# Results turned by VectorE in 32x32 blocks and stored in 128-byte runs; preparations split later

## The chip, the cores and the metric

One core of a Trainium2 chip. The metric is the device time of one execution in microseconds (us). The kernel before took 1075.37 us in the median of 3 runs (1073.84 to 1076.38). Engines: TensorE (PE in the profile, PEld for its weight loads), VectorE (DVE), ScalarE (ACT), GpSimd (POOL), SyncE (SP, which here only issues transfers).

## The reference, cut

```python
# q, k, v: (4, 8, 768, 64); gamma is one number for each head
for t in range(S):
    state = gamma * state + outer(k[t], v[t])
    y[t] = scale * q[t] @ state
x = y.transpose(0, 2, 1, 3).reshape(3072, 512)
h = x @ moe_w_in                                  # 512 -> 2048
x = maximum(0.01 * h, h) @ moe_w_out              # 2048 -> 512
h = x @ moe2_w_in
return (h * sigmoid(1.702 * h)) @ moe2_w_out      # (3072, 512) float32
```

A decayed linear attention, then two feed-forward layers, all in float32.

## The kernel before

The work runs in five stages, one after another on PE.

1. `retention()`: the attention, with the first block of the first input product between its steps (0 to 134 us of the trace).
2. The block loop: blocks 1 to 5 of the first input product. A block is 512 tokens, a tile `m` is 12 matmuls of 128x512 (`ffn_in`, L238) into one of six PSUM banks, and ACT empties the bank (L242). A call `later.tick()` ends a tile. Each float32 operand is kept as a rounded high part and a low part: ACT copies the high part, DVE subtracts (`split`, L154 and L151). `x_split(q, k)` does this for a quarter of the next block's input; it reads `x_raw`, and after the last quarter it issues the load of the block after (`x_load`, L205). In the same loop 36 weight preparations run (`Prep`), one started about every 1.78 tiles. A preparation loads its raw weights at tick 0, ACT and DVE turn them into float32 words and sums at tick 3 (`words`, `sums`: L172, L173, then L176 to L191 and L151). The first six (`keep`) and six later ones (`split`) also make the high and low parts at tick 4; stores go out at tick 6. The buffers for the sums, `rings[1]`, are three, so the words of the third preparation after one write where its sums stood.
3. `second1.run`: the first output product, 7 products in place of 8 for each 2x2 block (`Second`, L770).
4. `first2.run`: the second input product with the gate (`First`, L581).
5. `second2.run`: the second output product, three blocks of 56 items; an item is 6 matmuls of 128x512 (L770) with one `(blk, i, q)`. Operands are made four items ahead (`high` on ACT, L727; `low` on DVE, L151) in a ring of five tiles, so ACT may write the operand of an item once PE is done with the item five before. Raw rows are loaded 13 items ahead (`load`, L715, 256 KB each); sums of raw rows are made by DVE in the order of a table (`total`, L739).

A finished result of stage 5 is a tile `t` of 128 features by 2 x 512 tokens, so it is turned before it is stored. `evacuate` names four results for each block, S10, S11, S01 and S00 here, for (r, col) = (1,0), (1,1), (0,1), (0,0); they are turned at the ticks of items 43, 45 and 51 of their block and of item 1 of the next. Before the change `result2` has PE turn eight 128x128 pieces against `ident` into the PSUM banks of the result's tag (L994), ACT copies the banks to SBUF (L998), and one tick later SP issues one store of 512 KB with runs of 1 KB (L999). The last result of all goes through `last_result` (L1024 to L1036) and is not touched. Eleven results go through `result2`.

An SP instruction is issued in program order: a store that waits for its data holds the loads behind it. The tiles that hold results come from a ring of four (`second2.u`).

Of the kernel before, what the change touches and what calls it, by code (L numbers as in the profile page):

```python
# [21 lines left out]
P = 128  # L22
# [65 lines left out]
def retention_two_ffn(ctx: ExitStack, tc: tile.TileContext, qkv, consts, small, w1i, w1o, w2i, w2o, scratch, out):  # L88
    nc = tc.nc
    sbuf = ctx.enter_context(tc.tile_pool(name="sbuf", bufs=1, reuse_waits="tile"))  # L90
    banks = ctx.enter_context(tc.tile_pool(name="psum", bufs=1, space=PSUM)).tile([P, 8, TB], F32, name="psum")
# [24 lines left out]
    def run_of(area, n, step, at=0):  # L116
        return [(area, at + step * k) for k in range(n)]
# [11 lines left out]
    later = Later()  # L129
# [23 lines left out]
    def split(hi, lo, src, eng=nc.vector):  # L153
        nc.scalar.copy(out=hi, in_=src)  # L154
        subtract(lo, src, hi.bitcast(F32), eng)
# [48 lines left out]
    def x_load(q):  # L204
        nc.sync.dma_start(out=x_raw, in_=xd0[q])  # L205

    def x_split(q, k):
        split(xs[q % 2][k][:, 0], xs[q % 2][k][:, 1], x_raw[:, k])
        if k == NP - 1 and q + 1 < NB:
            x_load(q + 1)  # L210
# [20 lines left out]
    def ffn_in(blk, m, place=None):  # L231
        h = banks[:, h_banks[i_h[0] % len(h_banks)]]
        i_h[0] += 1
        w = wt[m].rearrange("p s (k f) -> p s k f", k=NP)
        i = 0
        for k in range(NP):
            for a, c in ((0, 1), (0, 0), (1, 0)):
                nc.tensor.matmul(out=h, lhsT=w[:, a, k], rhs=xs[blk % 2][k][:, c], start=(i == 0),  # L238
                                 stop=(i == 3 * NP - 1), skip_group_check=True)
                i += 1  # L240
        t = next(g_ring) if place is None else place
        nc.scalar.activation(out=t, in_=h, func=AF.Lrelu)  # L242
        if place is None:
            nc.scalar.dma_start(out=gd1[m][:, blk * TB : blk * TB + TB], in_=t)
# [159 lines left out]
    class Prep:  # L404
# [37 lines left out]
        def store(self):  # L442
            nc.sync.dma_start(out=wd[self.kind][:, self.q, self.hh], in_=self.t[:, 1:])
# [14 lines left out]
        def start(self, clock):  # L458
            self.load()
            split = self.kind == "2i" and self.q < N_SPLIT  # L460
            keep = self.kind == "1o" and self.q < 3
            clock.at(3, self.words)
            clock.at(3, self.sums)
            if split or keep:
                clock.at(4, self.split if split else self.keep)
            if not keep:
                clock.at(6, self.store_split if split else self.store)

        def steps(self):

# [14 lines left out]
    def w_load(kind, q, a, b):  # L485
        if kind == "2i" and q < N_SPLIT:
            nc.sync.dma_start(out=slot(q)[:, :, :, a:b], in_=wds[:, q, :, :, a:b])
        else:
            nc.sync.dma_start(out=slot(q)[:, :, 1, a:b], in_=wd[kind][:, q, :, a:b])
# [9 lines left out]
    def w_split(q, a, b):  # L499
        for hi, lo in w_parts(q, a, b):  # L500
            split(hi.bitcast(F32R), lo.bitcast(F32R), lo)
# [15 lines left out]
    class First:  # L517
# [46 lines left out]
        def run(self, done, step, behind):  # L564
# [9 lines left out]
            def product(t, n, i, start):  # L574
                blk, q = pairs[n]
                x = self.of[blk, i]
                w = slot(q).bitcast(F32R)[:, :, :, SLOTS["i"].index(i)]
                m = 0
                for k in range(2):
                    for a, b in ((0, 1), (0, 0), (1, 0)):  # L580
                        nc.tensor.matmul(out=t, lhsT=w[:, k, a], rhs=x[:, b, k], start=(start and m == 0),  # L581
                                         stop=(m == 5), skip_group_check=True)
                        m += 1
# [288 lines left out]
    for blk in range(1, NB):  # L872
        for m in range(KF):
            n = (blk - 1) * KF + m
            if given < min(N_IN1, (n + 1) * N_IN1 // 64):
                Prep(*names[given], prep_rings).start(later)
                given += 1
            if blk + 1 < NB:
                if m in (8, 9, 10, 11):
                    x_split(blk + 1, m - 8)  # L880
            elif m == 11:
                second1.begin(later, 2 * NQ, 2 * NQ, 3, 1)
            ffn_in(blk, m, second1.place(0, 1, *divmod(m, NQ)) if blk + 1 == NB else None)
            if blk + 1 == NB and m in freed:
                q = freed[m]
                for a, b in ((3, 7), (0, 3)) if m < 11 else ((6, 7), (3, 6), (0, 3)):
                    w_load("1o", q, a, b)
                if m < 11:
                    later.at(3, lambda q=q: w_split(q, 3, 7))
                    later.at(4, lambda q=q: w_split(q, 0, 3))  # L890
            later.tick()
# [14 lines left out]
    def done1(n, blk, i, q):  # L906
# [19 lines left out]
        if i == 2 and q < 3:  # L926
# [8 lines left out]
    second2 = Second({"x": run_of(x_a, 8, 2), "y": run_of(y_a, 8, 2), "z": run_of(z_a, 8, 2),  # L935
                      "ops": run_of(o_a[0], 4, 4) + run_of(o_a[1], 1, 4),
                      "u": run_of(u_a[0], 2, 4) + run_of(u_a[1], 2, 4)},
                     gd2, {"d": (4, 5), "e": (6, 7), "f": (0, 1), "h": (2, 3)})
# [42 lines left out]
    ident = Area("g").view(0, P)  # L981
# [4 lines left out]
    def result2(blk, r, col, t, tag, ticks=2):  # L986

        def turn():
            b0 = second2.p_banks[tag][0]
            y = banks[:, b0 : b0 + 2].rearrange("p j (b f) -> p (j b) f", f=2 * P).rearrange(  # L990
                "p b (j f) -> p b j f", j=2)
            for b in range(4):
                for j in range(2):
                    nc.tensor.matmul(out=y[:, b, j], lhsT=t[:, j, b * P : b * P + P], rhs=ident,  # L994
                                     is_transpose=True, start=(b % 2 == 0 and j == 0), stop=True,
                                     skip_group_check=True)
            s = next(second2.u).rearrange("p j (b f) -> p (j b) f", f=2 * P).rearrange("p b (j f) -> p b j f", j=2)
            nc.scalar.copy(out=s, in_=y)  # L998
            later.at(1, lambda: nc.sync.dma_start(  # L999
                out=out[second2.rows(blk, r)].rearrange("(b p) f -> p b f", p=P)[:, :, 2 * col * P : 2 * col * P + 2 * P],  # L1000
                in_=s.rearrange("p b j f -> p b (j f)")))

        later.at(ticks, turn)

# [104 lines left out]
```

## Time and profile before

| | us |
|---|---|
| median of 3 runs | 1075.37 (1073.84 to 1076.38) |
| the profiled execution's own time | 1073.59 |
| its span | 1071.5 |
| PE busy | 1052.3 (98%) |
| DVE busy | 816.0 (76%) |
| ACT busy | 585.4 (55%) |
| granted TensorE clock, mean | 0.998 |

All other numbers come from that one execution. Busy shares are means over five stages with different limits; a wait is read in its stage. A row of the chain of waits says what the time at that place was spent on; PE's chain rows are the pace at which its matmuls follow each other, which is shorter than the mean time of one.

### The profile page before, as it was taken

The page shows a single profiled execution, that of the slowest core. Times are in us where ns is not written, and L with a number is a line of the kernel's source. Part 1 is how long each engine was busy: PE and PEld are TensorE (multiplying, and loading weights), DVE is VectorE, ACT ScalarE, POOL GpSimd, SP SyncE. Part 2 cuts the span into 40 slices and gives each one's busy share as a digit, 9 for nine tenths or more (in the row PEclk, how much of TensorE's full clock was granted, in tenths as well). Part 3 has the DMA queues.
Part 4 walks back from the last instruction along what each step waited for, and adds up shares of the span by engine and source line. Part 5 has one row for each costly group of instructions (what it writes and reads, how often), then busy time and mean ns, then how long its engine had stood idle before and what let it go on. Part 6 is the DMA issues. An engine that isn't in the chain of part 4 may idle for free.

```text
span 1071.5 us, 16963 instructions
## 1 busy us (share of the span) xinstructions
PE 1052.3 (98%) x6042; PEld 902.4 (84%) x6043; DVE 816.0 (76%) x1380; ACT 585.4 (55%) x1116; POOL 93.3 (9%) x91
## 2 busy tenths in 40 slices
PE   8999999999899999999999999999999999999998
PEld 6777788887688888888888999999999788888886
DVE  5988737977796698787788767676867995885883
ACT  5866435645464554544545666465666555555553
POOL 2312100000000000000000104434300000000000
PEclk9999999999999999999999999999999999999999
DMA  9999665998896523525437936648387535335322
GB/s 342 348 396 337 213 228 188 314 316 302 294 350 227 172 80 128 187 79 177 138 123 280 354 121 228 222 157 307 122 316 257 183 99 197 102 96 197 107 70 79
DMA packets 128164, 225.81 MB, mean 211 GB/s; under 512 B 11088, under 2 KB 72784, under 8 KB 124752
## 3 DMA queue, kind: packets, MB, share of 16 engines
q1 hardware_dynamic: 97440, 178.29, 48.7%
q10 hardware_dynamic: 30640, 46.45, 11.7%
q8 instruction: 47, 0.77, 0.3%
q14 instruction: 37, 0.30, 0.1%
HBM read 138.71 MB, written 85.98 MB: 210 GB/s over the span
## 4 chain that ended last, share of the span: by engine, by line
PE 78%; DVE 8%; DMA 8%; ACT 3%; issue 2%; ACTq 0%; SPq 0%; DVEq 0%
PE psum L770 40%; PE psum L581 21%; PE psum L238 12%; DMA h<-qkv 2%; PE psum L277 1%; DMA b<-w1o 1%; PE psum L307 1%; DMA b<-gd 1%; DVE b L151 1%; PE psum L994 1%; DMA wd1o<-b 1%; DVE b L191 1%; DMA xd<-h 1%; PE psum L300 1%; DMA gd<-e 1%
## 5 line engine op out<-in xcount | busy, mean ns | idle before, releaser
L770 PE MATMUL psum<-c,h 128*128 128x512 f32 x1008 | 228.8, 389 | 0.0
L770 PEld LDWEIGHTS psum<-c,h 128*128 128x128 f32 x1008 | 189.2, 188 | 39.3
L770 PE MATMUL psum<-e,h 128*128 128x512 f32 x768 | 182.1, 391 | 1.0 <-DVE e L151 1.0
L770 PEld LDWEIGHTS psum<-e,h 128*128 128x128 f32 x768 | 143.3, 188 | 31.6 <-DVE e L151 1.3
L238 PE MATMUL psum<-d,h 128*128 128x512 f32 x576 | 138.2, 397 | 4.9 <-DVE d L151 3.3
L238 PEld LDWEIGHTS psum<-d,h 128*128 128x128 f32 x576 | 107.8, 190 | 31.1 <-DVE d L151 3.7
L238 PE MATMUL psum<-a,h 128*128 128x512 f32 x576 | 131.5, 389 | 0.0
L238 PEld LDWEIGHTS psum<-a,h 128*128 128x128 f32 x576 | 107.9, 188 | 23.0 <-ACT e L242 0.4
L581 PE MATMUL psum<-b,h 128*128 128x384 f32 x576 | 110.4, 334 | 2.1 <-ACT psum L654 2.1
L581 PE MATMUL psum<-c,h 128*128 128x384 f32 x576 | 110.1, 334 | 0.3 <-DVE d L618 0.3
L581 PEld LDWEIGHTS psum<-b,h 128*128 128x128 f32 x576 | 100.7, 188 | 2.8 <-ACT psum L654 2.8
L581 PEld LDWEIGHTS psum<-c,h 128*128 128x128 f32 x576 | 100.7, 188 | 0.6 <-DVE d L618 0.6
L727 ACT CAST c<-b 128x512 fp32r<-128x512 f32 x96 | 59.2, 622 | 57.1 <-DVE c L151 35.6
L601 ACT ACTIVATE d<-psum 128x384 f32<-128x384 f32 x96 | 47.1, 492 | 65.0 <-PE psum L581 54.8
L151 DVE TENSOR_TENSOR c<-b,c 128x512 fp32r<-128x512 f32 x96 | 65.4, 689 | 18.8 <-ACT c L727 16.6
L242 ACT ACTIVATE e<-psum 128x512 f32<-128x512 f32 x80 | 47.3, 591 | 42.7 <-PE psum L238 37.6
L727 ACT CAST e<-a 128x512 fp32r<-128x512 f32 x77 | 47.3, 622 | 41.6 <-PE psum L770 17.1
L151 DVE TENSOR_TENSOR h<-h 128x384 fp32r<-128x384 f32 (+2 forms) x80 | 44.9, 595 | 31.9 <-ACT h L154 20.4
L151 DVE TENSOR_TENSOR e<-a,e 128x512 fp32r<-128x512 f32 x77 | 52.3, 688 | 18.5 <-ACT e L727 17.1
L151 POOL TENSOR_TENSOR a<-a 128x768 f32<-128x768 f32 x7 | 13.2, 1891 | 509.4 <-DMA h<-wds 461.4
L605 DVE TENSOR_TENSOR d<-psum,d 128x384 f32<-128x384 f32 x96 | 52.1, 549 | 4.3 <-ACT d L601 3.6
L770 PE MATMUL psum<-f,h 128*128 128x512 f32 x192 | 49.0, 390 | 0.0
(148 smaller groups left out, 1469.6 us busy)
## 6 DMA issues: line engine op xcount, KB each, us to landing
gd<-d ACTq DMA_DIRECT2D x128, 192.0 KB, 3.6
h<-qkv SPq DMA_DIRECT2D x21, 1024.0 KB, 8.6
gd<-e ACTq DMA_DIRECT2D x80, 256.0 KB, 5.0
d<-gd SPq DMA_DIRECT2D x64, 256.0 KB, 3.8
b<-gd SPq DMA_DIRECT2D x64, 256.0 KB, 4.0
a<-gd SPq DMA_DIRECT2D x48, 256.0 KB, 5.1
c<-w1i SPq DMA_DIRECT2D x16, 512.0 KB, 7.7
xd<-e SPq DMA_DIRECT2D x12, 512.0 KB, 3.2
```

Of the source, the lines that this page charges most:

```text
L151: e.tensor_tensor(out=o, in0=x, in1=y, op=ALU.subtract)
L191: e.tensor_tensor(out=f.bitcast(I32), in0=f.bitcast(I32), in1=low.bitcast(I32), op=ALU.add)
L238: nc.tensor.matmul(out=h, lhsT=w[:, a, k], rhs=xs[blk % 2][k][:, c], start=(i == 0), stop=(i == 3 * NP - 1), skip_group_check=True)
L242: nc.scalar.activation(out=t, in_=h, func=AF.Lrelu)
L277: nc.tensor.matmul(out=ps[:, e, n], lhsT=kT[r, n], rhs=qT[r, n], start=True, stop=True, skip_group_check=True)
L300: nc.tensor.matmul(out=kv[r, n], lhsT=ks[:, 2 * n + e], rhs=v[:, n, r], start=(c == 0 and n == 0), stop=True, skip_group_check=True)
L307: nc.tensor.matmul(out=out(n, e), lhsT=v[:, n, r], rhs=sm[:, e, n], start=(n < 2), stop=(c == 0), skip_group_check=True)
L581: nc.tensor.matmul(out=t, lhsT=w[:, k, a], rhs=x[:, b, k], start=(start and m == 0), stop=(m == 5), skip_group_check=True)
L601: nc.scalar.activation(out=s, in_=src, func=AF.Sigmoid, scale=1.702)
L605: nc.vector.tensor_tensor(out=dst, in0=src, in1=s, op=ALU.mult)
L727: nc.scalar.copy(out=t[:, 0], in_=self.block_of(*item))
L770: nc.tensor.matmul(out=t[:, j], lhsT=w[:, j, a], rhs=x[:, b], start=(new and q == 0 and m == 0), stop=(q == NQ - 1 and m == 2), skip_group ...
```

## The change

```diff
@@ Prep.start
             if split or keep:
-                clock.at(4, self.split if split else self.keep)
+                clock.at(6, self.split if split else self.keep)
             if not keep:
-                clock.at(6, self.store_split if split else self.store)
+                clock.at(7 if split else 6, self.store_split if split else self.store)
@@ the block loop
             if blk + 1 < NB:
-                if m in (8, 9, 10, 11):
-                    x_split(blk + 1, m - 8)
+                if m in (2, 4, 6, 8):
+                    x_split(blk + 1, m // 2 - 1)
@@ result2
         def turn():
-            b0 = second2.p_banks[tag][0]
-            y = banks[:, b0 : b0 + 2].rearrange("p j (b f) -> p (j b) f", f=2 * P).rearrange(
-                "p b (j f) -> p b j f", j=2)
-            for b in range(4):
-                for j in range(2):
-                    nc.tensor.matmul(out=y[:, b, j], lhsT=t[:, j, b * P : b * P + P], rhs=ident,
-                                     is_transpose=True, start=(b % 2 == 0 and j == 0), stop=True,
-                                     skip_group_check=True)
-            s = next(second2.u).rearrange("p j (b f) -> p (j b) f", f=2 * P).rearrange("p b (j f) -> p b j f", j=2)
-            nc.scalar.copy(out=s, in_=y)
-            later.at(1, lambda: nc.sync.dma_start(
-                out=out[second2.rows(blk, r)].rearrange("(b p) f -> p b f", p=P)[:, :, 2 * col * P : 2 * col * P + 2 * P],
-                in_=s.rearrange("p b j f -> p b (j f)")))
+            s = next(second2.u)
+            nc.vector.transpose(out=s, in_=t)
+
+            def store():
+                o = out[second2.rows(blk, r)][:, 2 * col * P : 2 * col * P + 2 * P].rearrange(
+                    "(c a) (j i b) -> i j a c b", a=32, j=2, i=4)
+                for i in range(4):
+                    for j in range(2):
+                        nc.sync.dma_start(out=o[i, j], in_=s[32 * i : 32 * i + 32, j].rearrange("p (c b) -> p c b", b=32))
+
+            later.at(2, store)
```

DVE turns each 32x32 block in place of PE's 128x128 pieces, in one instruction for a result. A block then lies on 32 partitions, so a result goes out in eight stores of 64 KB, each of 32 partitions by 16 runs of 128 bytes, two ticks after the turn. In stage 2 the high and low parts of a preparation are made at tick 6, a split preparation is stored at tick 7, and the input of the next block is split at tiles 2, 4, 6 and 8.

SP's queue in stage 5 at the end of its first block, before (y is the output, a, b and d are raw rows):

```order
L715 DMA a<-gd_78 128x512 x2
L999 DMA y<-c_7422 128x4x256
L715 DMA a<-gd_78 128x512 x2
L999 DMA y<-c_7108 128x4x256
L715 DMA a<-gd_78 128x512 x4
L715 DMA b<-gd_78 128x512 x2
L999 DMA y<-c_7108 128x4x256
L715 DMA b<-gd_78 128x512 x6
L999 DMA y<-c_7422 128x4x256
L715 DMA d<-gd_78 128x512 x8
```

The same place of SP's queue now:

```order
L715 DMA a<-gd_78 128x512 x3
L997 DMA y<-c_7422 32x16x32 x8
L715 DMA a<-gd_78 128x512 x2
L997 DMA y<-c_7108 32x16x32 x8
L715 DMA a<-gd_78 128x512 x3
L715 DMA b<-gd_78 128x512 x3
L997 DMA y<-c_7108 32x16x32 x8
L715 DMA b<-gd_78 128x512 x5
L715 DMA d<-gd_78 128x512
L997 DMA y<-c_7422 32x16x32 x8
L715 DMA d<-gd_78 128x512 x7
```

Each store became eight, and one load more stands ahead of each result.

DVE in stage 5 at the same block end, the difference (e and f are operands of PE, c the results):

```order
 L778 TENSOR_TENSOR c_7108<-c_7422,c_7108 128x1024
-L151 TENSOR_TENSOR e<-a,e 128x512 x2
-L151 TENSOR_TENSOR e<-b,e 128x512
+L151 TENSOR_TENSOR e<-a,e 128x512
+L990 STREAM_TRANSPOSE c_7422<-c_7422 128x1024
+L151 TENSOR_TENSOR e<-a,e 128x512
+L151 TENSOR_TENSOR e<-b,e 128x512
+L990 STREAM_TRANSPOSE c_7108<-c_7108 128x1024
 L151 TENSOR_TENSOR f<-b,f 128x512
 L151 TENSOR_TENSOR e<-b,e 128x512 x3
```

Turns now stand between the subtractions for PE's operands; the other results' turns stand alike.

ACT in stage 2, from the words of one split preparation (c) to the copy of its high part (f), before:

```order
L172 ACTIVATE c_1600<-c_1600 128x512
L173 ACTIVATE c_1600<-c_1600 128x512
L154 CAST d<-c_81 128x512
L242 ACTIVATE e<-psum 128x512
L244 DMA gd_77<-e 128x512
L154 CAST f<-c_1600 128x896
```

The same preparation's rows on ACT now:

```order
L172 ACTIVATE c_1604<-c_1604 128x512
L173 ACTIVATE c_1604<-c_1604 128x512
L242 ACTIVATE e<-psum 128x512
L244 DMA gd_77<-e 128x512
L154 CAST e<-b 128x896
L242 ACTIVATE e<-psum 128x512
L244 DMA gd_77<-e 128x512
L172 ACTIVATE b<-b 128x512
L173 ACTIVATE b<-b 128x512
L242 ACTIVATE e<-psum 128x512
L244 DMA gd_77<-e 128x512
L154 CAST f<-c_1604 128x896
```

The copy moved back behind three tiles and the next preparation's words; the input's copies (d) left this place.

## Rows read from the trace of the kernel before

**Rows 1.** The page's part 1: busy us, share of the span, instructions.
```profile
span 1071.5 us, 16963 instructions
PE 1052.3 (98%) x6042; PEld 902.4 (84%) x6043; DVE 816.0 (76%) x1380; ACT 585.4 (55%) x1116; POOL 93.3 (9%) x91
```

**Rows 2.** The page's part 4: the chain that ended last, by line.
```profile
PE psum L770 40%; PE psum L581 21%; PE psum L238 12%; DMA h<-qkv 2%; PE psum L277 1%; DMA b<-w1o 1%; PE psum L307 1%; DMA b<-gd 1%; DVE b L151 1%; PE psum L994 1%; DMA wd1o<-b 1%; DVE b L191 1%; DMA xd<-h 1%; PE psum L300 1%; DMA gd<-e 1%
```

**Rows 3.** Stages 2, 5: us, busy PE, PEld, DVE, ACT, POOL (count), clock, DMA share, GB/s.
```profile
132.00:356.00 224.00, 219.13 (x980) 179.60 (x979) 156.64 (x328) 111.93 (x192) 0.00 (x0) 0.99 0.77 269
...
856.00:1072.00 216.00, 211.53 (x980) 175.28 (x978) 158.89 (x242) 107.33 (x169) 0.00 (x0) 1.00 0.36 117
```

**Rows 4.** The chain in order of time, stage 5: start, us, what.
```profile
887.59 0.87 PE psum L994 x8
...
910.22 57.17 PE psum L770 x252
...
1057.17 0.96 PE psum L994 x8
```

**Rows 5.** Line 994 by itself: minimum/median/maximum ns.
```profile
L994 PE MATMUL psum<-g,c x88: 270/272/301, 887.4 to 1057.9; 128*128 128x128 f32 x88
```

**Rows 6.** PE in stage 2, timeline: start, us; in brackets idle before and releaser.
```profile
266.53 2.34 PE L238 MATMUL psum<-d,h 128*128 128x512 f32 x9 [1.33 <-ACT e L242]
272.18 10.76 PE L238 MATMUL psum<-d,h 128*128 128x512 f32 x39 [3.31 <-DVE d L151]
283.17 32.93 PE L238 MATMUL psum<-d,h 128*128 128x512 f32 x144 [0.23 <-ACT e L242]
```

**Rows 7.** ACT's waits for sums of split preparations, stage 2: us in total, times, longest.
```profile
ACT f L154 <- DVE b L151: 6.6, 2, 3.7
...
ACT e L154 <- DVE b L151: 5.3, 2, 2.9
...
ACT e L154 <- DVE c L151: 3.3, 1, 3.3
...
ACT f L154 <- DVE c L151: 2.4, 1, 2.4
```

**Rows 8.** Groups by line and shape in stage 5: busy us, mean ns, idle before.
```profile
L151 DVE TENSOR_TENSOR e<-a,e 128x512 fp32r<-128x512 f32 x64 | 43.6, 689 | 18.5 <-ACT e L727 17.1
L727 ACT CAST e<-a 128x512 fp32r<-128x512 f32 x64 | 39.3, 622 | 35.8 <-PE psum L770 14.6 <-DVE e L151 13.4 <-DVE f L151 4.4
...
L778 DVE TENSOR_TENSOR c<-c,c 128x1024 f32<-128x1024 f32 x3 | 3.7, 1217 | 0.0
```

**Rows 9.** Transfers from 1059 to 1063.5 us (one store, 1 KB runs): packets, MB, share.
```profile
q1 hardware_dynamic: 528, 0.52, 33.3%
```

**Rows 10.** Transfers from 1068 to 1071.5 us (512-byte runs): packets, MB, share.
```profile
q1 hardware_dynamic: 272, 0.13, 13.2%
```

**Rows 11.** Transfers from 2 to 4.6 us (288-byte reads on q10): packets, MB, share.
```profile
q10 hardware_dynamic: 144, 0.04, 7.9%
```

**Rows 12.** SP's timeline behind two stores of stage 5.
```profile
902.25 0.39 SPq L999 DMA_DIRECT2D y<-c  x1
902.69 3.44 SPq L715 DMA_DIRECT2D b<-gd  x6
...
911.74 4.41 SPq L715 DMA_DIRECT2D d<-gd  x8
```

**Rows 13.** Transfers by line: KB each, median us from issue to landing.
```profile
b<-gd SPq DMA_DIRECT2D x64, 256.0 KB, 4.0
...
wds<-b SPq DMA_DIRECT2D x4, 448.0 KB, 5.0
```

**Rows 14.** DVE's timeline: the sum that reads the second b row of its block.
```profile
908.83 0.68 DVE L739 TENSOR_TENSOR a<-b,a 128x512 f32<-128x512 f32 x1
```

**Rows 15.** The end of the program, timeline: DVE and ACT.
```profile
1045.43 1.22 DVE L778 TENSOR_TENSOR c<-c,c 128x1024 f32<-128x1024 f32 x1
...
1068.43 0.39 ACTq L1036 DMA_DIRECT2D y<-c  x1
```

## The prediction

> **What bounds the kernel now.** I read busy times first, then the chain of waits, then the stages. PE is busy for 1052.3 of 1071.5 us, DVE for 816.0 [rows 1], and the chain is mostly PE's three matmul lines, with the turns, L994, as one of its smaller items [rows 2]. So time is won where PE has work to lose or waits to lose, and lost where a new wait reaches PE. The change touches two stages. In stage 5 PE is busy for 211.53 of 216 us with DVE at 158.89, ACT at 107.33 and the transfers at 36% [rows 3]: PE bounds, DVE has 57 us spare, the DMA engines most of their time. In stage 2 PE is busy for 219.13 of 224 us, and the rest is three waits near the start of block 4: 1.33 us for ACT to free a bank, 3.31 us for DVE's split of the input, 0.23 us for ACT again [rows 6].
>
> **The change part by part.**
>
> *PE's turns, removed.* 88 matmuls in 11 results [rows 5]. In the chain the eight of a result cost 0.87 us, the last eight 0.96 [rows 4]; PE runs them between its products without a gap, so all of it is on the path: 10 x 0.87 + 0.96 = **9.7 us less**. ACT loses 11 copies, for which PE did not wait: nothing on the path.
>
> *DVE's turns, added.* The trace has no such operation. Nearest is DVE's pass over the same 1024 float32 elements from SBUF to SBUF, 1.217 us; half the width takes 0.689 us, my lower bound [rows 8], and twice the 1.217, 2.4 us, is the upper. I take 1.2 us: 11 x 1.2 = 13.2 us (bounds 7.6 and 26.8) against 57 us spare. Queued behind a turn on DVE are the subtractions for PE's operands. Their margin: an operand may be written once PE has four items left before it, 24 matmuls at 57.17 / 252 us, 5.4 us [rows 4], less 0.62 for the copy and 0.69 for the subtraction [rows 8]: about 4 us. One turn and one subtraction in an item of 1.36 us cost 1.9 us: 0.5 us of delay, made good in the next item. At 2.4 us the delay is 1.7 us. Hidden either way; if the margin were gone, the 13.2 us would come back to PE.
>
> *The stores.* Eleven of 512 packets of 1 KB become 88 of 512 packets of 128 bytes. The price of a packet is the question of this case. A 1-KB packet takes 0.333 x 4.5 us x 16 engines / 528 = 45 ns [rows 9], a 512-byte one 0.132 x 3.5 x 16 / 272 = 27 ns [rows 10]; 512 bytes less are 18 ns less, so the line through both gives 13.5 ns at 128 bytes. The mean over 128 reads of 288 bytes and 16 completion posts is 0.079 x 2.6 x 16 / 144 = 23 ns [rows 11], but in a crowd of other loads. From below I take 9 ns, the line's end at no bytes; from above, 27 ns. I take the line's 13.5, because both of its points are stores to this output; a result then is 4096 x 13.5 / 16 = 3.5 us of the engines (2.3 to 7.0) in place of 1.4. Issuing: eight transfers in a row took SP 4.41 us [rows 12], so I take 4.4 us of SP for a result instead of 0.39. At the taken price SP is the slower of the two, and a load behind a result goes out some 4 us later.
>
> Who waits for that? The tightest load is the fourth b row, now the first behind S01; its sum stands three items after the sum at 908.83 [rows 14], at 908.83 + 4.1 = 912.9, with the turn between them gone. S01 can be ready a little before the old store at 902.25, since one pass replaces a turn and a copy; I take 901.4. That plus 4.4 for the stores, 0.6 for its own issue and 4.0 to land [rows 12, 13] is 910.4. That is 2.5 us early, and DVE may be 4 us late before PE waits. The loads behind it are issued 0.6 us apart and needed 2.0 us apart. At block ends: nothing.
>
> At the very end, on the old clock: S10 can go out at 1046.7 (the block's last sum ends, [rows 15]) + 0.7 + 1.2 = 1048.6, S11 behind it until 1057.4, S01 until 1062.3. PE reaches its last results 2.6 us earlier than before (three turns of this block), so the last issue moves from 1068.4 [rows 15] to 1065.8, after SP and the engines are free. Nothing; the bound is rival A's.
>
> *Stage 2.* For the six split preparations ACT waited 6.6 + 5.3 + 3.3 + 2.4 = 17.6 us for their sums, up to 3.7 us at a time [rows 7], because the copy stood one tile behind its words. Each wait held the emptying of PE's banks and the input's copies behind it, and that lag is what PE met at 266.5 and 272.2 [rows 6]. A tile is 32.93 / 12 = 2.7 us [rows 6]; two more tiles, 5.5 us, cover 3.7, so these waits go. The input's last quarter has eight tiles (22 us) in place of five until its block begins, so the lag would have to grow by 8 us to be met. New is that the words of the third preparation behind, on average at tick 8.3, write where the sums are still being stored: copied and subtracted by tick 6.8, landed 5.0 us later [rows 13], near tick 8.7 or 9. ACT may wait 1 to 2 us there, six times, 6 to 11 us against 17.6. I take all three PE waits as gone: **4.9 us less**; bounds 0 and 4.9, and a loss only if ACT's lag passes the 13 us of five spare banks, which a smaller sum of waits excludes for these. What is late next: nothing, since PE runs from 283 us on without a wait [rows 6].
>
> **The sum.** 1073.6 (the profiled execution, 2.1 us more than its span) - 9.7 - 4.9 = 1059.0. That execution was 1.8 us under the median of 1075.4, so in the median **1061 us**.
>
> **The rivals.**
>
> *A. Short writes cost more than 512-byte ones.* Place: the DMA engines between S10 and the d loads at the two inner block ends, and between S10 and the last store of the program. For it: no row shows a 128-byte write to memory. Against it: the line of rows 9 and 10. Up to about 22 ns the loads come in time. At 27 ns a result is 7 us: S10 from 890 to 897, S11 to 904, the eight loads before S01 (0.65 us each by the same line) to 909, S01 to 916, and the fourth b row lands near 917.5. Due it is at 911 (of 912.9 two earlier turns are gone), DVE stands, and past its 4 us PE waits some 3 us, with the d rows 4. At the end 24 stores of 0.87 us from 1048.6 on last to 1070, some 4 us too long. Together 2 x 4 + 4 = 12 of 14.6 us: it decides at **about 28 ns**. At 54 ns, a 512-byte packet paid twice, a result is 13.9 us: the same count gives some 33 us at each inner block end and 26 at the end, 1059 + 66 + 26 = 1151, in the median **1153 us**, slower than before.
> The Trainium skill, DMA: Bandwidth & Descriptors (Specifications), speaks for this rival: it asks for at least 512 bytes for line rate and says that below this the transfer becomes a read-modify-write. No run here shows that; by that rule the time would be this rival's 1153, by the line it is 1061.
>
> *B. The waits of stage 2 come back.* The store at tick 7 and the three buffers put ACT as far behind as before. For it: a store's landing against the ticks, above. Against it: 17.6 us of waits become 6 to 11. It gives 1061 + 4.9 = **1066 us**.
>
> *C. Between the line and the break-even,* at 22 to 28 ns: 1061 to 1075, say **1068 us**.
>
> **How the numbers follow.** The forecast has 0.60, B 0.12, C 0.11, A 0.17. The forecast's own range is 1058 to 1064: runs of one kernel differ by 2.5 us, and a part of stage 2 may stay. To leave no more than 0.2 out, the range goes on over B and most of C: 1058 to 1069. Faster by over 0.2% (2.2 us, about what a measurement of this kernel can tell from no change): 0.60 + 0.12 + 0.08 = 0.80; within it 0.03; slower 0.17.
>
> **What would show it.** In the profile after, L994 is gone and PE's idle time in stage 5 stays near 4 us; a turn on DVE takes near 1.2 us; the packets of a result take 3.5 us of each engine, and SP issues eight stores in about 4.4 us; no sum (L739) waits for a load for more than 4 us; the last store is issued near 1054 us. In stage 2 PE has no wait above 0.3 us, and the copies of the split preparations wait for no sum. It is wrong if the sums wait for b or d rows at the block ends and PE behind them, or if the program ends on the stores of S01: that is A, and the packet's price, read from the transfers of such a stretch, says how far.

## The result and the profile of the changed kernel

The changed kernel takes **1062.84 us** in the median of four runs (1062.0 to 1064.63), the kernel before 1075.67 us in four runs beside it (1073.84 to 1076.38). The ratio is 0.9889, with a 95% interval of 0.9871 to 0.9906: 12.8 us less. The profiled execution took 1063.07 us and its span is 1061.4 us, against 1071.5 us in [rows 1].

Read in the same order as before. The page's part 1, which answers [rows 1]:

```profile
span 1061.4 us, 16876 instructions
...
PE 1041.0 (98%) x5955; PEld 893.4 (84%) x5955; DVE 825.5 (78%) x1391; ACT 579.2 (55%) x1105; POOL 93.5 (9%) x91
```

PE has 11.3 us less work, DVE 9.5 us more. The stages, which answer [rows 3] (stage 5 now ends sooner, so its stretch is 10 us shorter; the columns are those of [rows 3]):

```profile
132.00:356.00 224.00, 224.00 (x1013) 185.12 (x1012) 160.79 (x337) 119.06 (x200) 0.00 (x0) 1.00 0.80 274
856.00:1062.00 206.00, 196.05 (x868) 161.75 (x866) 163.90 (x244) 95.75 (x155) 0.00 (x0) 0.99 0.48 121
```

In stage 2 PE has no idle time at all. In stage 5 it has 10 us, and nearly all of that lies behind its last matmul, as the end's timeline shows further down.

**Stage 2.** PE's timeline, which answers [rows 6] (start, duration, count; no idle time in brackets any more; `...` stands for rows left out):

```profile
136.06 43.82 PE L238 MATMUL psum<-a,h 128*128 128x512 f32 x192
...
266.75 43.68 PE L238 MATMUL psum<-d,h 128*128 128x512 f32 x192
...
353.79 2.43 PE L770 MATMUL psum<-c,h 128*128 128x512 f32 x10
```

The five blocks take 353.79 - 136.06 = 217.7 us. Before they took 359.46 - 134.05 = 225.4 us, so the stage gives 7.7 us although its three waits summed to 4.9. The windows of the kernel before, from the end of its longest wait on, show where most of the rest was (busy PE, PEld, DVE, ACT, POOL; then the granted clock, the DMA share and GB/s):

```profile
272.00:274.00 2.00, 1.82 (x6) 1.45 (x7) 1.60 (x4) 2.00 (x4) 0.00 (x0) 0.73 0.43 57
274.00:276.00 2.00, 2.00 (x6) 1.53 (x5) 1.79 (x4) 0.73 (x2) 0.00 (x0) 0.50 0.88 303
```

PE stood for 3.31 us, and when it went on the granted clock was 0.73 and 0.50, and 0.92 in the 2 us after these, so part of the time at 1.2 instead of 2.4 GHz. The 39 matmuls of [rows 6] took 10.76 us where 39 of the block of 192 take 39 x 43.68 / 192 = 8.9 us: 1.9 us of clock behind a wait of 3.3.

ACT's waits in stage 2 (us in total, times, longest), which answer [rows 7]:

```profile
ACT b L172 <- DMA wds<-b: 11.7, 2, 9.4
...
ACT c L172 <- DMA wds<-c: 3.4, 1, 3.4
...
ACT f L154 <- DVE b L180: 0.9, 2, 0.5
```

The 17.6 us of waits of the split preparations' copies are down to 2.2, the largest of them the 0.9 shown. ACT waits 15.1 us for the stores of sums instead, in three waits of up to 9.4 us: the new wait that the prediction named. PE's banks were empty in time all the same. Six more waits are gone, which the prediction did not count: the copies of the six kept preparations had stood for 16.3 us before (tile h of L154, 2.4 to 3.3 us each, between 150 and 187 us), and PE had met no wait behind those. So what a wait of ACT costs PE does not follow from its length.

**Stage 5.** DVE's turns by line and shape, and what DVE's sums wait for (the second fence: us in total, times, longest):

```profile
L990 DVE STREAM_TRANSPOSE c<-c 128x1024 f32<-128x1024 f32 x11 | 13.6, 1237 | 0.0
```

```profile
DVE a L739 <- DMA b<-gd: 5.3, 4, 2.2
```

A turn takes 1.24 us. The sums wait for loads by up to 2.2 us, which they never did before, but PE does not wait behind them. The rows of SP and DVE at the first block end show for which loads; below them stand S01's eight stores (shortest, median and longest in ns, first and last start):

```profile
894.88 1.33 SPq L715 DMA_DIRECT2D b<-gd  x3
...
896.30 6.89 SPq L997 DMA_DIRECT2D y<-c  x8
...
900.44 0.69 DVE L739 TENSOR_TENSOR a<-b,a 128x512 f32<-128x512 f32 x1 [1.90 <-DMA b<-gd]
...
906.46 0.69 DVE L739 TENSOR_TENSOR a<-b,a 128x512 f32<-128x512 f32 x1 [0.59 <-DMA b<-gd]
```

```profile
L997 SPq DMA_DIRECT2D y<-c x8: 382/498/2037, 896.3 to 902.7; - x8
```

The longer wait is for the first b row, issued at 894.88 behind S11; the fourth, issued at 903.29 behind S01, costs 0.59 us. The second block end is alike, with 2.20 and 0.58 us. S01's eight stores take SP 6.89 us, where S10's take 4.18: two of them took 2.04 and 1.59 us in place of some 0.5, while the last a row and the three b rows were landing. SP has no wait for a completion in front of any of the eight; what held the two is not shown.

PE in stage 5, its first row of the changed kernel and of the kernel before, then its last row in the kernel before (that of the changed kernel stands under "The end"):

```profile
850.16 4.38 PE L770 MATMUL psum<-e,h 128*128 128x512 f32 x18 [0.49 <-DVE e L151]
```

```profile
855.56 4.38 PE L770 MATMUL psum<-e,h 128*128 128x512 f32 x18 [0.53 <-DVE e L151]
...
1067.28 0.71 PE L1028 MATMUL psum<-g,c 128*128 128x128 f32 x4 [0.46 <-ACT c L1024]
```

From the start of stage 5 to the last matmul PE takes 1052.53 - 850.16 = 202.4 us, against 1068.01 - 855.56 = 212.45 us: 10.1 us less (the ends are those of the chain, 0.02 us behind the timeline's). The transfers from 884 to 888 us, nothing but stores of one result (packets, MB, share of 16 engines):

```profile
q1 hardware_dynamic: 3667, 0.46, 66.1%
```

A packet of 128 bytes takes 0.661 x 4 us x 16 / 3667 = 11.5 ns.

**The end.** SP's timeline, and below it SP's waits from 1030 us on:

```profile
1035.75 22.08 SPq L997 DMA_DIRECT2D y<-c  x24
1057.93 0.97 SPq L1034 DMA_DIRECT2D y<-c  x2
```

```profile
SPq L997 <- DMA y<-c: 9.5, 2, 7.0
```

and ACT's two stores of the last result there, with PE's last matmuls:

```profile
1049.00 0.40 ACTq L1034 DMA_DIRECT2D y<-c  x1
...
1052.95 0.40 ACTq L1034 DMA_DIRECT2D y<-c  x1
```

```profile
1051.80 0.71 PE L1026 MATMUL psum<-g,c 128*128 128x128 f32 x4 [0.46 <-ACT c L1022]
```

The 24 stores of the last block take SP 22.08 us, of which it stands for 9.5 us, until a transfer to y is complete. PE is done at 1052.5 and the span ends 8.9 us later, against 3.5 us before. The listing of the compiled program tells which transfer it is (row, line, tile, shape, what the instruction waits for):

```text
SP   538 L997  DMA y<-c_7108 32x16x32  [waits DMAHW6_49]
SP   539 L997  DMA y<-c_7108 32x16x32  [waits DMAHW7_49]
SP   540 L997  DMA y<-c_7108 32x16x32  [waits DMAHW0_49,DVE_49]
ACT 1102 L1034 DMA y<-c_7422 128x2x128 [waits DMAHW7_49,Activation_49]
```

All transfers of SP and ACT share eight completion semaphores, and each of SP's stores waits until the previous user of its own is complete. When the program was built, semaphore 7 went to ACT's tail store first and to the last store of S11 (row 539) after it. SP comes to row 539 some 5 us before ACT can issue its tail store at 1049.0, and everything queued behind row 539 on SP, all of S01 and SP's half of the tail, stands until that store has landed. The same happens in S01 with ACT's second tail store. The times agree: ACT's two stores landed 1.85 us after their issue, at 1050.85 and 1054.80, and these are SP's rows from there on:

```profile
1050.87 1.40 SPq L997 DMA_DIRECT2D y<-c  x3
```

```profile
1054.81 3.02 SPq L997 DMA_DIRECT2D y<-c  x6
```

So the profile adds up: stage 1, whose code is the same, ended 2.0 us later in this execution (PE waited 1.79 us for a load of q, k and v at 68.4 us, 0.54 at the same place before, and the granted clock was 0.50 from 70 to 72 us); stage 2 took 7.7 us less; stages 3 and 4 0.3 us more; PE's part of stage 5 10.1 us less; the end 5.4 us more. 2.0 - 7.7 + 0.3 - 10.1 + 5.4 = -10.1 = 1061.4 - 1071.5.

### The profile page after: what moved, and what is told of

The parts are those of the page before. It is cut to its first block, busy times and chain, and to the rows that moved or that the text cites. A ratio compares the mean times of both kernels' runs of the same rounds, so it can differ in the third digit from the quotient of the medians.

```text
span 1061.4 us, 16876 instructions
## 1 busy us (share of the span) xinstructions
PE 1041.0 (98%) x5955; PEld 893.4 (84%) x5955; DVE 825.5 (78%) x1391; ACT 579.2 (55%) x1105; POOL 93.5 (9%) x91
## 4 chain that ended last, share of the span: by engine, by line
PE 90%; DVE 4%; DMA 3%; issue 1%; ACT 1%; SPq 0%; ACTq 0%; DVEq 0%
PE psum L770 40%; PE psum L238 24%; PE psum L581 20%; PE psum L277 2%; PE psum L307 2%; DMA h<-wd2o 1%; PE psum L300 1%; DMA b<-gd 1%; DMA h<-qkv 1%; PE psum L313 1%; DVE b L180 1%; DMA a<-gd 0%; PE psum L370 0%; DVE b L280 0%; DVE e L151 0%
```

## The experiments

**e1: the tail from one queue.** The suspected wait is taken away by its cause: ACT issues no store at the end.

```diff
-            (nc.sync, nc.scalar)[k].dma_start(out=y[:, 2 * k : 2 * k + 2], ...
+            nc.sync.dma_start(out=y[:, 2 * k : 2 * k + 2], ...
```

> The changed kernel with one edit: all four of the last result's stores go out from SP, none from ACT. Theory: in the changed kernel SP's last stores wait for the completion of ACT's two tail stores, with which they share completion semaphores (SP stood 7.0 us, then about 2.5 us more); without that the 24 block stores go out without a gap from about 1036 on, are done near 1052, and the span ends 3.5 to 4.5 us after PE in place of 8.9: 1062.8 - 5 = 1058 us, bounds 1057 to 1059.5. Rival: the 24 stores take 22 us because SP and the DMA engines can do no better; then the wait only moves, and the time stays at 1062 to 1064 us.

Measured: 1057.33 us (1056.37 to 1057.68), ratio to the kernel before 0.9832 (0.981 to 0.9854). SP's timeline at the end:

```profile
1035.59 13.10 SPq L997 DMA_DIRECT2D y<-c  x24
```

The 24 stores take 13.1 us in place of 22.1. PE ends at 1052.3, as in the changed kernel, and the span at 1055.9, 3.6 us behind it. The theory's 5 us are there; the stores themselves are not what is slow.

**e9: the tail's second half from POOL.** e1 takes away both the shared semaphore and the second engine that stores at the same time. This edit takes away only the first: POOL's transfers have no semaphore in common with SP's.

```diff
-            (nc.sync, nc.scalar)[k].dma_start(out=y[:, 2 * k : 2 * k + 2], ...
+            (nc.sync, nc.gpsimd)[k].dma_start(out=y[:, 2 * k : 2 * k + 2], ...
```

> The changed kernel with one edit: the two tail stores that ACT issued are issued by POOL, which here has no completion semaphore in common with SP's stores; two engines still store at the same time, as in the changed kernel. Theory (SP waits for the completion of a store with which its own shares a semaphore): SP issues its 24 block stores in about 13 us from 1036 on, as in e1, and is done near 1049 in place of 1058; the end is set by POOL's own last store, whose price no run shows: 1057 to 1060 us. Rival (two queues that store at once hold each other up): SP still stands 7 to 10 us before the tail, 1062 to 1064 us.

Measured: 1057.28 us (1056.73 to 1058.52), ratio 0.9848 (0.9828 to 0.9867). Timelines of SP and of POOL:

```profile
1034.23 13.08 SPq L997 DMA_DIRECT2D y<-c  x24
```

```profile
1047.76 0.86 POOL L1034 DMA_DIRECT2D y<-c  x1 [229.42 <-ACT c L1033]
```

Two engines store at once, and the 24 stores take 13.08 us, as in e1. It is the shared semaphore that costs the 5 us.

**e2 and e3: each half of the change alone.** e2 has only the new function for the results, e3 only stage 2's three lines.

> The kernel before with only the results changed (DVE's transpose and 128-byte stores); stage 2 as before. Theory of the trace after: PE's stage 5 gives 10 us, the end takes 5 back: 1075.4 - 10.1 + 5.4 = 1070.7 us, with PE's waits of 1.3 and 3.3 us in stage 2 as before. By the prediction's own terms (turns 9.7, end nothing): 1065.7 us. Rival (the two parts depend on each other): anything outside 1065 to 1072.

> The kernel before with only stage 2 changed (input splits in an earlier tile, preparations' split two tiles later, their store one later); results as before. Prediction's term, the three waits alone: 1075.4 - 4.9 = 1070.5 us. Theory of the trace after: the 3.3 us wait also costs clock behind it (granted 0.50 to 0.92 for some 6 us), so 1075.4 - 7.7 = 1067.7 us; granted clock about 1.0 in every stretch of stage 2.

Measured: e2 1070.14 us (1067.86 to 1072.38), ratio 0.9954 (0.9935 to 0.9972); e3 1067.46 us (1065.51 to 1070.16), ratio 0.9927 (0.9907 to 0.9948); the kernel before had 1074.59 us beside both. So e2 gives 4.5 us and e3 7.1 us, 11.6 together, close to the 12.8 of the whole change: the parts are independent, and both came out where the theory of the trace put them. The price of the end sits in e2: 4.5 is near 10.1 - 5.4 = 4.7, not the 9.7 of the turns, and its 24 last stores take SP 22.10 us. And e3's gain is nearer to 7.7 than to 4.9. One window shows why, of e2 first, of e3 second, the same 4 us:

```profile
272.00:276.00 4.00, 3.42 (x8) 2.74 (x9) 3.41 (x6) 3.13 (x5) 0.00 (x0) 0.58 0.53 145
```

```profile
272.00:276.00 4.00, 4.00 (x19) 3.31 (x18) 2.40 (x5) 0.39 (x1) 0.00 (x0) 1.00 0.96 350
```

e2 still has the wait for DVE, 3.31 us, and behind it PE does 8 matmuls at a granted clock of 0.58; e3 does 19 at 1.00.

**e5 and e6: stage 2 taken apart.** e5 moves only the preparations' split and store to later ticks, e6 only the input's quarters to earlier tiles.

```diff
e5:
-                clock.at(4, self.split if split else self.keep)
+                clock.at(6, self.split if split else self.keep)
-                clock.at(6, self.store_split if split else self.store)
+                clock.at(7 if split else 6, self.store_split if split else self.store)
e6:
-                if m in (8, 9, 10, 11):
-                    x_split(blk + 1, m - 8)
+                if m in (2, 4, 6, 8):
+                    x_split(blk + 1, m // 2 - 1)
```

> The kernel before with only the preparations moved (split two tiles later, their store one later); the input's quarters split where they were. Prediction's reading: ACT's waits for the preparations' sums are the lag that PE meets, so this half alone takes all three waits of PE away: 1074.6 - 7.1 = 1067.5 us, as stage 2 whole. Rival: the input's quarters are late by themselves (four of them between tiles 8 and 11, the last one five tiles ahead of its use), so the 3.3 us wait for DVE's split stays, and its clock with it: 1074.6 - 1.5 = 1073 us.

> The kernel before with only the input's quarters split in tiles 2, 4, 6 and 8 in place of 8 to 11; preparations as before. Prediction's reading: ACT still waits some 17 us for the preparations' sums, so PE still waits for ACT (1.3 and 0.2 us), while the 3.3 us for the input's last quarter go, with the clock behind them: 1074.6 - 3.3 - 2.8 = 1068.5 us. Rival: it is the sums' waits alone that matter, and the 3.3 us stay in another place: 1074 to 1075 us.

Measured, beside a kernel before of 1074.9 us: e5 1068.09 us (1065.16 to 1070.22), ratio 0.9937 (0.9917 to 0.9957); e6 1070.51 us (1069.49 to 1071.06), ratio 0.9961 (0.9946 to 0.9976). PE's waits in block 4, e5 first, then e6:

```profile
278.26 32.93 PE L238 MATMUL psum<-d,h 128*128 128x512 f32 x144 [1.28 <-ACT e L242]
```

```profile
267.00 5.74 PE L238 MATMUL psum<-d,h 128*128 128x512 f32 x24 [0.66 <-ACT e L242]
274.63 38.42 PE L238 MATMUL psum<-d,h 128*128 128x512 f32 x168 [1.88 <-ACT e L242]
```

Either half alone removes the 3.31 us, and the loss of clock with it. Neither alone removes all waits for ACT: e5 leaves one of 1.28 us, e6 two of 2.5 us together. By PE's start of the next stage, the five blocks of stage 2 take 217.7 us with both halves, 354.55 - 135.24 = 219.3 with e5, 356.40 - 135.49 = 220.9 with e6, 225.4 with neither. Both theories of e5 miss in part (the waits don't all go, and the 3.3 us don't stay), and e6 comes out near its first, but with 2.5 us of waits left instead of 1.5.

**e4, e7, e8: how much room the stores have.** All three start from e1 and cut the stores of the first two blocks, eight results, finer. e7 cuts each store into two of 256 packets, still of 128 bytes; e8 into two of 512 packets of 64 bytes; e4 into four of 512 packets of 32 bytes. Bytes and results are the same in all.

```diff
e7 (`source` is the old store's in_):
+                        w = 8 if blk + 1 < NB2 else 16
+                        for k in range(0, 16, w):
+                            nc.sync.dma_start(out=o[i, j][:, k : k + w], in_=source[:, k : k + w])
e8 (e4: 8 in place of 16):
+                        w = 16 if blk + 1 < NB2 else 32
+                        for k in range(0, 32, w):
+                            nc.sync.dma_start(out=o[i, j][:, :, k : k + w], in_=source[:, :, k : k + w])
```

> As e1, but in the first two of the three blocks each result is stored in runs of 32 bytes: 16384 packets and 32 stores in place of 4096 and 8. Line through 512-byte and 1-KB packets (9 ns + 0.035 ns a byte): 10 ns a packet, 10 us of each engine for a result; SP at 0.55 us an issue 17.6 us. The fourth b row then goes out some 13 us later at each inner block end and lands near 924 where its sum is due at 911 to 913; 4 us are covered, so PE waits 6 to 10 us at each of two block ends, 1058 + 12 to 20 = 1070 to 1078 us. Rival A's price (short writes paid twice, 54 ns and no less for 32 bytes): 55 us of each engine for a result, over 1150 us. Rival: cover is far larger than counted, and PE does not wait: 1058 us.

> As e1, but in the first two of the three blocks each of the eight stores of a result is cut in two: 16 stores of 256 packets, packets of 128 bytes and their number as in e1. Theory: SP's issue, near 0.5 us a store whatever its size, is the cost that grows; a result takes SP 7 to 8 us, its b rows go out about 3 us later after each of three results at a block end, and PE, with some 4 us covered, waits 2 to 8 us at each of two block ends: 1057.3 + 4 to 16 = 1061 to 1073 us. Rival: SP's time goes by packets, 8.4 ns of SP each, and a result still takes 4.2 us: 1057 us.

> As e7 in its 16 stores a result, but each of 512 packets of 64 bytes, twice the packets of e7. If SP's issue per store sets the cost, this comes out within 2 us of e7; a packet then takes 8 to 9 ns (7.3 measured at 32 bytes in e4, 11.5 at 128). If the packets set it, it loses about twice what e7 loses against e1: SP 8.4 us a result against 4.2, 1065 us or more with e7 at 1057.

Measured: e7 1078.47 us (1077.56 to 1079.74), ratio 1.0036 (1.0024 to 1.0049); e8 1086.87 us (1084.08 to 1090.95), ratio 1.0118 (1.0086 to 1.0149); e4 1158.09 us in one run. SP's timeline for the same three steps at the first block end, in e1, e7 and e8: the stores of S10, the stores of S01, and (but in e8) the loads behind S01, the first of which brings the fourth b row:

```profile
883.15 4.15 SPq L997 DMA_DIRECT2D y<-c  x8
...
896.20 7.04 SPq L997 DMA_DIRECT2D y<-c  x8
903.34 2.35 SPq L715 DMA_DIRECT2D b<-gd  x5
```

```profile
881.87 7.74 SPq L1000 DMA_DIRECT2D y<-c  x16
...
901.44 9.73 SPq L1000 DMA_DIRECT2D y<-c  x16
911.26 2.29 SPq L715 DMA_DIRECT2D b<-gd  x5
```

```profile
880.71 8.30 SPq L1000 DMA_DIRECT2D y<-c  x16
...
901.68 12.18 SPq L1000 DMA_DIRECT2D y<-c  x16
```

A store costs SP 4.15 / 8 = 0.52 us with 512 packets and 7.74 / 16 = 0.48 us with 256; with 512 of 32 bytes, in e4, the 32 stores of S10 take 16.80 us, 0.53 each. So SP's time goes by stores and hardly by packets. The transfers from 884 to 888 us, e8 first, then e4:

```profile
q1 hardware_dynamic: 3851, 0.24, 51.2%
```

```profile
q1 hardware_dynamic: 4137, 0.13, 46.9%
```

A packet takes 0.512 x 4 x 16 / 3851 = 8.5 ns at 64 bytes and 0.469 x 4 x 16 / 4137 = 7.3 ns at 32. The DMA engines are half idle in both; SP is what the stores wait for. What PE then waits for from 845 us on in e7 (us in total, times, longest):

```profile
PE psum L770 <- DVE e L151: 13.0, 6, 6.2
PE psum L770 <- DVE f L151: 1.6, 1, 1.6
```

In e7 the first b row behind S11 is issued at 900.0 in place of 894.8 in e1 and the fourth at 911.3 in place of 903.3. PE, which in e1 waited for 0.5 us, waits for 14.6; its two longest waits, 3.26 and 6.20 us, stand behind sums that wait 7.33 and 10.27 us for the first b row, the second of them here (DVE, then PE):

```profile
992.59 0.69 DVE L739 TENSOR_TENSOR a<-b,a 128x512 f32<-128x512 f32 x1 [10.27 <-DMA b<-gd]
```

```profile
993.93 7.27 PE L770 MATMUL psum<-e,h 128*128 128x512 f32 x18 [6.20 <-DVE e L151]
```

PE's waits in e4 are 85.9 us. Behind the 6.20 us of e7 the granted clock is down, as in stage 2 of the kernel before; it is 0.50 from 905 to 910 us as well, behind the wait of 3.26:

```profile
995.00:1000.00 5.00, 5.00 (x13) 3.89 (x12) 3.01 (x5) 1.12 (x2) 0.00 (x0) 0.50 0.39 61
```

e7's span is 21.7 us longer than e1's, and PE's stretch from its wait at the start of stage 5 to its last matmul 23.0: 14.1 us more of waits, and 8.9 more in matmuls, most of it at the lower clock (the 24 behind the wait of 3.26 us took 8.44 us in place of 5.60). So twice the stores eat all that the change gives, and the kernel is slower than before. The expected 4 to 16 us for e7 held for the waits and left the clock out. The forecast for e4 moved the fourth b row back by one result's stores, where three results are queued ahead of it: it went out 36 us later than in e1, at 939.65. That e4's 1158 us agrees with the "over 1150" of rival A's price is chance: that price is 54 ns a packet, and the packets took 7.3. e8 was expected within 2 us of e7 if SP's issue alone counts, and is 8.4 us above it: its stores take SP 8.3 us when nothing else is under way, near e7's 7.7, but 12.2 against 9.7 us where loads run beside them. So of the 29.5 us by which e8 is slower than e1, 21.1 come with the number of stores (e7); the rest comes with their packets, and how is not shown.

**e10: the turn done twice.** From e1, with the transpose line of each result repeated. The turn is in place, so the second one puts the blocks back: the time is that of twice the turns, and the results stored are not turned.

```diff
             nc.vector.transpose(out=s, in_=t)
+            nc.vector.transpose(out=s, in_=t)
```

> As e1, with each of the 11 transposes by DVE done twice into the same tile: 13.6 us more of DVE, 2.5 us a turn. Prediction: at 2.4 us a turn the subtraction behind it comes 1.7 us late of 4 us of cover, so nothing in the middle; at the very end S01's store goes out about 1.2 us later and still before the tail: 1057.3 us, bounds 1056 to 1059. Rival: the cover on DVE is used up by the sums that already wait for loads (up to 2.9 us in e1), and each doubled turn costs PE about 1.2 us: 1057.3 + 8 to 13 = 1065 to 1070 us.

Measured: 1063.1 us (1059.98 to 1064.46), ratio 0.9894 (0.987 to 0.9917). PE's waits from 845 us on:

```profile
PE psum L770 <- DVE e L151: 2.0, 3, 1.1
PE psum L770 <- DVE d L151: 0.5, 1, 0.5
```

That is 2.0 us more than e1, and PE's way from its wait of 0.5 us at the start of stage 5 to its last matmul is 3.4 us longer (852.83 to 1058.65 us, against 849.88 to 1052.34). So of 13.6 us more on DVE most is hidden, but not all: of the three new waits two, of 0.40 and 1.13 us, lie at the block ends, where the sums already wait for loads, and one of 0.53 among the last products. The median is 5.8 us above e1's. In the profiled execution 2.2 of 6.6 us are stage 1, which ended at 137.40 in place of 135.17 us; how much of the median is that stage's own scatter, with four runs from 1060 to 1064.5, stays open. Neither theory holds as written; the prediction's "hidden" is nearer for the waits.

## Why the prediction was right, and where it was not

The time forecast was 1061 us and came out at 1062.8, inside the range and inside the forecast's own range. But two of its terms were off, and in opposite directions.

- **PE's turns: right.** 9.7 us forecast. PE's part of stage 5 is 10.1 us shorter.
- **DVE's turn: right.** 1.24 us against 1.2. It costs nothing as changed. At twice its length it begins to reach PE (e10, 2 us of waits), where the prediction said "hidden either way".
- **The packet: right.** 11.5 ns against 13.5 taken. The line through the 1-KB and 512-byte stores was a little high, and the packets get cheaper below it (8.5 ns at 64 bytes, 7.3 at 32). Rival A's doubled price is ruled out for 128, 64 and 32 bytes. The Trainium skill, DMA: Bandwidth & Descriptors (Specifications), asks for at least 512 bytes for line rate and says that below this a transfer becomes a read-modify-write. The first half agrees with these prices, by which 16 engines would move 16 x 512 / 27 = 303 GB/s at 512 bytes and 16 x 128 / 11.5 = 178 at 128. Of the second no row here shows a price: a packet takes less time below 512 bytes, not more, and the measurement decides.
- **Loads at the block ends: right result, wrong row.** PE met no wait, as forecast, but the sums did. The prediction took the fourth b row, the first load behind S01, for the tightest and had it 2.5 us early; its sum waits 0.59 us, so 3.1 us are missing. Two steps failed. "4.4 for the stores" was 6.9 for S01. And the due time of 912.9 left out the two earlier turns that rival A's working does count (911): DVE came to the sum at 906.46 - 0.59 = 905.87, which is 911.3 on the old clock, since stage 5 begins 5.4 us earlier here. A landing sooner than taken gave some of this back. Tighter still was the first b row, which the prediction did not look at: it landed 5.5 and 4.8 us after its issue at the two block ends, 4.0 were taken, and its sums wait 1.90 and 2.20 us. The 4 us of cover on DVE were right: in e7 PE's two longest waits are each 4.07 us shorter than those of the sums ahead of them. e7 also shows how little is left: 3.6 us more per result, and PE waits for 14.6 us.
- **Stage 2: mechanism right, term mis-sized.** 4.9 us forecast, 7.7 measured in the profile, 7.1 by e3. The waits were counted, but not the matmuls behind them: 1.9 us at the lower clock, and some 0.9 us for three restarts (in e5 the one wait of 1.28 us makes the stage 1.6 us longer than without, so 0.3 a restart). The bound of 4.9 from above was therefore wrong. The attribution was half right: ACT's lag behind the sums is a cause, since e5 removes the long wait (though the six kept preparations' waits, as long, had cost PE nothing), but the input's late quarters are another, since e6 removes it as well, and both halves are needed for PE to run through. Rival B did not come: ACT waits 15.1 us on the stores, more than the 6 to 11 forecast, and PE does not notice.
- **The very end: wrong.** "Nothing" was forecast, 5.4 us were lost. The step added up SP's and the engines' time for 24 stores and found both free before the tail, which is so (13.1 us in e1, done at 1048.7). It left out that SP's stores wait on completion semaphores shared with ACT's, in an order fixed at build time. Its sign for this step, a last store issued near 1054 us, failed: 1058.5 in the changed kernel, 1053.0 in e1. (Its 1062.3 for S01 should be 1057.4 + 4.4 = 1061.8; nothing hangs on that.) The kernel before had the same eight semaphores, and SP met no such wait there: its three last block results were three transfers, not 24.

Against the working on the profiled execution, 1059.0: stage 2 gave 2.8 us more than forecast, PE's turns 0.4 more, the end took 5.4, stages 1, 3 and 4 came out 2.3 us longer without a change in their code, and what lies around the span 0.4 shorter: 1059.0 - 2.8 - 0.4 + 5.4 + 2.3 - 0.4 = 1063.1. So the forecast was near partly by luck: its two misses offset each other.

e1, one line from the changed kernel, beats both: 0.983 of the time before, 0.981 to 0.9854, an interval that lies below that of the changed kernel.

## What to carry to other kernels

When one store becomes eight, count the issuing queue before the packets: here the queue's half microsecond a store, and the loads behind it, decide, while the engines were busy for 66% of a stretch of nothing but stores. At the end of a program look at which transfers share completion semaphores across queues: a store that can be issued early may be made to wait for one that can't. And a wait of PE is worth more than its length when the granted clock is down behind it, so read the clock in the windows after the wait before its removal is priced; the length of the wait alone did not tell here.

## What was not expected of the hardware

- Stores in short runs are cheap for the DMA engines: 11.5 ns a packet at 128 bytes, 8.5 at 64, 7.3 at 32, against 45 at 1 KB [rows 9] and 27 at 512 [rows 10].
- A store costs SP about 0.5 us to issue, with 256 packets (0.48) or 512 (0.52). Beside loads that are landing a single one took up to 2.04 us (S01 in the changed kernel).
- The granted clock was down to 0.50, 1.2 of 2.4 GHz, after PE had stood for 3.31 us in stage 2 of the kernel before, and around waits of 3.26 and 6.20 us in e7; in e5 and e6 it stayed at 1.00 behind waits of 1.28 and 1.88 us. But it also was 0.50 behind a wait of 1.79 us in stage 1 of the changed kernel (70 to 72 us) and behind one of 1.81 us in e7 (1018 to 1020 us), so the length of the one wait does not decide.
- Stage 1 of the same code ended anywhere from 134.05 (kernel before) to 137.40 us (e10) in the profiled executions: more than some of the effects studied here, and a reason to compare stage by stage.
